# A new order of steps in a two-layer MoE kernel after Nystrom attention

## The chip, the cores and the metric

The kernel runs on one core of a Trainium2 chip. Its time is device microseconds of one execution, as a median over runs. The engines are TensorE (PE, with its weight loads PEld), VectorE (DVE), ScalarE (ACT), GpSimd (POOL) and SyncE (SP), which here only issues transfers. Each has a queue of its own that it works off in order; semaphores hold an instruction back until what it reads has been written and what it overwrites has been read.

## The reference

Inputs are q, k, v of 4 batches, 8 heads, 576 positions and 64 channels, and four weight matrices. First comes Nystrom attention with 32 landmarks, then two dense layers over 2304 tokens (512 channels, 2048 hidden):

```python
A, Bm, C = sm(q, k_lm), sm(q_lm, k_lm), sm(q_lm, k)     # scaled softmax; *_lm: means over 18 positions
Z = Bm.T / (norm1(Bm) * norminf(Bm) + 1e-6)
for _ in range(6): Z = 2 * Z - Z @ Bm @ Z
x = tokens(A @ Z @ C @ v)                                # 2304 x 512
h = x @ w_in;  x = (h * tanh(softplus(h))) @ w_out       # layer 1
h = x @ w2_in; out = square(maximum(h, 0)) @ w2_out      # layer 2
```

## The kernel before

All products of the two layers are made of three passes: each operand is split in a high part (a rounded copy, ScalarE) and a low part (the difference, GpSimd or VectorE), and PE adds high x high, high x low and low x high. Layer 2 moreover uses a scheme of seven products in place of eight on two by two blocks, so that VectorE makes many sums and differences of blocks.

The order of everything is written out by hand in one string, PROGRAM, of 2638 steps, and a loop runs through it and calls for each step one method, which emits the step's few instructions. A step reads `thing.method`, with a number, then `@` and the kind of PSUM buffer that it takes, then `+n`: so many products with the identity go ahead of the next step that takes a PSUM buffer. As every engine works in order, the place of a step in the string sets its place in its engine's queue. It also sets which buffer it gets: a buffer of each kind goes to the next step that asks, in the order in which buffers were given back.

The things that matter here:

- `a` to `h`: groups of heads of the attention; `B0` to `B2`: the iteration for Z; `F`: attention folded into the first weights.
- `U0` to `U63`: 128 rows or columns of a weight matrix; `d` loads them (SP), `lo`, `st`, `ab`, `cl`, `ad` convert them on ScalarE, VectorE and GpSimd, `hi` and `lw` split them, `sv` stores them to DRAM (SP).
- `p0` to `p31`: chunks of 288 tokens of layer 1's hidden part: `f` products, `M` the activation and `c` the high part (ScalarE), `g` the low part (VectorE). `t0` to `t23`: turns of 384 tokens of its second product: `y` on PE (L931 to L933), `e` adds on VectorE (L1016).
- `W0` to `W7`: pairs of layer 2's first weights: `v` sums (VectorE, L1031), `h` high parts (ScalarE, L1039), `l` low parts (GpSimd, L1043), `sv` stores to DRAM (SP, L1051 to L1056), which gives the buffers back. There are four buffers of this kind, "T". `K0` to `K7` do the same for the second weights.
- `X0` to `X2`: the forms of layer 1's output, for three passes of 768 tokens: `t` (VectorE), `h` (ScalarE, L1077), `l` (L1082).
- `Q00` to `Q27` (pass, then pair): the first product of layer 2. `a` loads a 256 KB weight (SP, L1273), `p` is a product (PE, L1284 to L1286, six matmuls), `s` and `d` move its result out of PSUM (ScalarE L1294, VectorE L1314). In pass 0 `r`, `h`, `g` make the activation and its parts, and `y` is the second product (PE, L1357 to L1359); `Q07.e` copies its sums (L1368), and `Q07.o` stores them (SP, L1376).
- `Y10` to `Y22`: the second product of passes 1 and 2: `r` the activation and `t` the sums (VectorE, L1150, L1155), `h` (ScalarE, L1173), `l` (GpSimd, L1178), `b` loads a 256 KB weight (SP, L1184), `p` is a product (PE, L931 to L933, 18 matmuls), `a` adds it to the totals (L1201, L1204).
- `Z1`, `Z2`: the endings of the passes: `u` sums (L1224), `f` (L1234, L1237), `e` and `o` stores.
- `x.e` and `x.m` load ScalarE's tables ahead of use.

The loads `a` and `b` and the split weights share 24 buffers of kind "w"; a load waits until the PE step that last read its buffer is done.

Of the kernel before, what the change touches and what calls it, by code (L numbers as in the profile page):

```python
# [10 lines left out]
F32 = mybir.dt.float32  # L11
F32R = mybir.dt.float32r
U32 = mybir.dt.uint32
# [41 lines left out]
    U0.cl U3.lo B0.n0@at B0.r0 B0.z0 U8.d U4.cl U3.st U4.ad B0.n1@y b.ae U3.ab B0.r1 B0.z1 c.xq U8.lo U4.hi U4.lw c.zq
    b.su U3.cl B0.n2@at B0.r2 B0.z2 b.pe@h c.TL c.pc@h+1 b.ET d.lk d.sk b.mu c.pb@at B0.n3@y B0.r3 b.lv B0.z3 b.pv@y
    U3.ad c.PB b.tb B0.n4@y B0.r4 e.lk c.pa@at B0.z4 c.cm B0.n5@y e.lq c.ce c.at B0.z5 d.tk@h+2 d.Sk b.ah d.tl@y
    e.tk@h c.am e.sq b.cv c.mi d.Tk B0.pw@y B0.wz d.TL U7.ab d.pc@at U5.d U5.lo d.cm c.pe@h e.Tk U0.ad d.pb@y d.PB
    c.ae F00.fo@h+1 B1.bx B1.be d.lv U5.st B1.bs B1.nr@y+1 b.al d.ce d.pe@at U8.st U5.ab B1.rs B1.n0@y U5.cl B1.z0
    F00.mh c.ET F00.ml f.lk f.tk@h U8.ab d.ET U6.d@gh B1.r0 U6.lo U6.st d.pa@at c.cr d.at B1.n1@y B1.z1 U7.cl f.Tk  # L60
    U5.ad U5.hi U6.ab e.Sq B1.r1 U6.cl U6.ad p0.f0 p0.f1 p0.f2 p0.M0 B1.n2@y B1.z2 B1.r2 p0.f3 p0.M1 p1.f0 U7.ad
    B1.n3@y g.lv U6.hi U6.lw d.am f.lq f.sq B1.r3 B1.z3 e.tq@h f.tq@at U7.hi e.Tq e.sk c.lv f.Tq B1.n4@y B1.r4 U7.lw
    B1.z4 p0.c0 p0.g0 d.pv@y f.lv p0.c1 d.cr e.Sk p1.f1 p1.M0 f.Sq c.pv@y c.cv c.su B1.n5@at x.m p1.f2 B1.z5 U5.lw
    e.tl@y p1.c0 p1.g0 p1.f3 p0.g1 d.cv B1.pw@y e.TL e.pb@at B1.wz p1.M1 p1.c1 e.pc@h e.PB F10.fo@h U11.d U11.lo U8.cl
    U8.ad p1.g1 t0.y0 F10.mh t0.y1 d.mi d.ae f.sk e.cm f.Sk e.ce f.tl@at t0.e0 d.su e.pe@h f.TL f.pb@y f.pa@at U9.d
    U9.lo F10.ml t0.e1 U11.st c.mu c.tb c.ah U11.ab f.PB U9.st U9.ab d.mu d.tb d.ah c.al f.pc@h f.cm f.ce t0.y2 t0.e2
    t0.y3 e.ET t0.e3 d.al p2.f0 p2.f1 U11.cl U11.ad g.lq f.at f.am U9.cl e.pa@at e.at p2.M0 p2.c0 p2.g0 g.lk p2.f2
    p2.f3 U9.ad p2.M1 p2.c1 p3.f0 e.am p3.f1 p2.g1 t1.y0 p3.M0 p3.c0 U10.d U10.lo U10.st p3.f2 U10.ab U10.cl g.tk@at
    g.Tk U13.d g.sk t1.e0 U13.lo U10.ad U13.st t1.y1 f.pe@h f.ET t1.y2 F01.fo@h t1.e1 g.Sk U13.ab e.mi e.ae g.tq@at
# [30 lines left out]
    t12.e1 t12.y2 U29.d U29.lo U29.st U35.d U29.ab U35.lo U35.st U35.ab W0.l0 W0.sv0 p18.M0 W0.h1 W0.l1 t12.y3 t12.e3  # L100
    U35.cl p18.M1 p18.c0 p18.g0 p18.c1 U35.ad p19.f0 W0.sv1 p19.f1 p19.f2 p19.f3 t12.e2 p19.M1 F22.fo@at F22.mh p18.g1
    U29.cl U41.d t13.y0 t13.e0 F22.ml W1.v0 W1.v1 W1.h0 p19.M0 p19.c0 t13.y1 t13.e1 U29.ad U29.hi W1.v3 U29.lw W1.v2
    p20.f0 W1.l0 W1.sv0 t13.y2 t13.y3 U40.d p19.g0 F32.fo@at p19.c1 p19.g1 U41.lo t13.e3 W1.h1 W1.l1 W1.sv1 U41.st
    U41.ab t14.y0 t14.e0 p20.f1 p20.f2 t13.e2 p20.f3 U41.cl p20.M0 t14.y1 t14.y2 F32.mh F32.ml p20.c0 p20.g0 U40.lo
# [1355 lines left out]
```

## Time and profile before

| | |
|---|---|
| median of 3 runs | 809.32 us (808.58 to 809.92) |
| profiled execution | 807.2 us |
| its span | 805.4 us |
| mean granted PE clock | 0.993 |
| busy: PE, DVE, ACT, POOL | 771.5, 608.6, 374.9, 383.3 us |
| transfers | 156.73 MB, mean 195 GB/s |

Attention and layer 1 take roughly the first half of the span, layer 2 the second. The busy time of PE is modelled from starts, so two matmuls that follow each other overlap in it; the idle time before an instruction, with the engine that ended it, is what to read for waits.

### The profile page before, as it was taken

How to read it: one execution, taken by the hardware profiler on the slowest of the kernel's cores; microseconds unless marked ns; L12 is line 12 of the kernel's file. 1: busy time of each engine (PE TensorE's matmuls, PEld its weight loads, DVE VectorE, ACT ScalarE, POOL GpSimd, SP SyncE). 2: the span in 40 equal slices, each digit the busy share in tenths (PEclk: the TensorE clock that was granted, in tenths of full speed). 3: DMA queues.
4: the chain of work that ended last, by engine and by line, in shares of the span. 5: the costliest groups of instructions: out<-in, count | busy, mean ns of one | idle time of the engine just before them, and what ended most of it. 6: DMA issues, size and time to landing. Idle time of an engine off the chain costs nothing.

```text
span 805.4 us, 15441 instructions
## 1 busy us (share of the span) xinstructions
PE 771.5 (96%) x5938; PEld 712.9 (89%) x5938; DVE 608.6 (76%) x964; ACT 374.9 (47%) x622; POOL 383.3 (48%) x265
## 2 busy tenths in 40 slices
...
GB/s 329 214 194 142 109 138 110 54 31 75 131 79 88 127 160 164 216 213 252 204 173 254 292 270 256 290 305 267 220 251 281 218 248 210 169 252 306 329 81 79
DMA packets 87721, 156.73 MB, mean 195 GB/s; under 512 B 9184, under 2 KB 37088, under 8 KB 87648
## 3 DMA queue, kind: packets, MB, share of 16 engines
...
## 4 chain that ended last, share of the span: by engine, by line
PE 69%; DVE 12%; POOL 7%; issue 6%; ACT 3%; DMA 2%; SPq 0%; POOLq 0%; ACTq 0%; DVEq 0%
PE y L931 7%; PE y L933 7%; PE y L932 7%; PE P L1284 5%; PE P L1285 5%; PE P L1286 5%; PE hc L931 4%; PE hc L932 3%; PE hc L933 3%; PE O L932 3%; PE O L931 3%; PE O L933 3%; PE O L1359 3%; PE O L1358 3%; PE O L1357 3%
## 5 line engine op out<-in xcount | busy, mean ns | idle before, releaser
L1178 POOL TENSOR_TENSOR ringglx<-A,ringghx 128x768 fp32r<-128x768 f32 x40 | 76.2, 1923 | 63.6 <-ACT ringghx L1173 60.1
L932 PE MATMUL O<-b,ringghx 128*128 128x256 f32 x240 | 68.6, 286 | 3.7 <-DMA b<-sc 3.7
L982 DVE TENSOR_TENSOR ringglx<-sc,ringghx 128x576 fp32r<-128x576 f32 (+2 forms) x80 | 60.1, 775 | 14.8 <-ACT ringghx L977 14.6
L931 PE MATMUL O<-b,ringghx 128*128 128x256 f32 x240 | 68.4, 285 | 1.7 <-DVE sum L1204 1.7
L933 PE MATMUL O<-b,ringglx 128*128 128x256 f32 x240 | 68.6, 286 | 1.1 <-POOL ringglx L1178 1.1
L1016 DVE TENSOR_TENSOR acc<-acc,y 128x384 f32<-128x384 f32 x72 | 39.0, 547 | 36.8 <-PE y L933 36.6
L964 ACT ACTIVATE sc<-hc 128x576 f32<-128x576 f32 x64 | 41.7, 652 | 51.1 <-PE hc L933 31.4
L1173 ACT CAST ringghx<-A 128x768 fp32r<-128x768 f32 x40 | 32.8, 836 | 69.6 <-PE O L932 22.7
L1314 DVE TENSOR_TENSOR U<-U,P 128x384 f32<-128x384 f32 x72 | 39.6, 551 | 33.8 <-PE P L1286 32.2
L932 PEld LDWEIGHTS O<-b,ringghx 128*128 128x128 f32 x240 | 46.5, 194 | 4.0 <-DMA b<-sc 4.0
L977 ACT CAST ringghx<-sc 128x576 fp32r<-128x576 f32 (+2 forms) x80 | 44.2, 578 | 12.2 <-PE y L933 11.4
L1314 DVE TENSOR_TENSOR A<-U,P 128x384 f32<-128x384 f32 x56 | 30.2, 548 | 25.8 <-PE P L1286 21.3
L931 PEld LDWEIGHTS O<-b,ringghx 128*128 128x128 f32 x240 | 46.4, 193 | 2.1 <-issue 2.0
L933 PEld LDWEIGHTS O<-b,ringglx 128*128 128x128 f32 x240 | 46.5, 194 | 1.3 <-POOL ringglx L1178 1.3
L404 POOL TENSOR_TENSOR wi<-rawwi 128x512 int32<-128x512 int32 x16 | 20.3, 1271 | 47.2 <-DVE rawwi L398 38.4
L1294 ACT COPY U<-P 128x384 f32<-128x384 f32 x24 | 11.5, 480 | 63.8 <-PE P L1286 53.9
L1204 DVE TENSOR_TENSOR sum<-sum,O 128x768 f32<-128x768 f32 x32 | 30.1, 949 | 10.5 <-PE O L933 10.4
L1155 DVE TENSOR_TENSOR A<-A,A 128x768 f32<-128x768 f32 x28 | 34.4, 1227 | 2.3 <-POOL ringglx L1178 1.8
L1150 DVE SCALAR_TENSOR_TENSOR A<-A 128x768 f32<-128x768 f32 x28 | 35.7, 1298 | 0.3
L418 POOL TENSOR_TENSOR rawwo<-rawwo 128x512 int32<-128x512 int32 x14 | 16.9, 1207 | 35.9 <-DVE rawwo L398 27.2
L411 POOL TENSOR_TENSOR wa<-rawwi 128x512 int32<-128x512 int32 x16 | 17.4, 1093 | 30.8 <-DVE rawwi L398 24.5
L384 DVE SCALAR_TENSOR_TENSOR rawwi<-rawwi 128x512 uint32<-128x512 uint32 x32 | 24.3, 764 | 10.0 <-ACT rawwi L381 10.0
...
## 6 DMA issues: line engine op xcount, KB each, us to landing
...
```

What stands on the lines that cost most here:

```text
L931: nc.tensor.matmul(ps, wh, rh, start=start, stop=False)
L932: nc.tensor.matmul(ps, wh, rl, start=False, stop=False)
L933: nc.tensor.matmul(ps, wl, rh, start=False, stop=stop)
L964: nc.scalar.activation(s, self.hs[hf][:, :, :CH], AF.Mish)
L977: nc.scalar.copy(self.at_ring("gh", hf, c0, e - a), self.s[hf][:, :, a:e])
L982: nc.vector.tensor_tensor(lo, self.s[hf][:, :, a:e], hi.bitcast(F32), ALU.subtract)
L1016: nc.vector.tensor_tensor(a, a, ps, ALU.add)
L1178: nc.gpsimd.tensor_tensor(lo, self.A[self.src(k)], hi.bitcast(F32), ALU.subtract)
L1284: nc.tensor.matmul(ps[:, :TT], wh[:, c], xh[:, c, :], start=c == 0, stop=False)
L1285: nc.tensor.matmul(ps[:, :TT], wh[:, c], xl[:, c, :], start=False, stop=False)
L1286: nc.tensor.matmul(ps[:, :TT], wl[:, c], xh[:, c, :], start=False, stop=c == 1)
L1314: nc.vector.tensor_tensor(to, x, self.ps[i][:, :TT], ALU.add)
```

## The change

The string PROGRAM is replaced by another with the same 2638 steps, each with the same kind of PSUM buffer; the methods and all else stay as they are. The numbers behind `+` stand at other places (before, 13 products with the identity in all; after, 19). On PE a step moves by 1.4 places in the mean and 17 at most; VectorE's by 2.9 and 37, GpSimd's by 1.7 and 20, SP's by 11.7 and 128. ScalarE changes its tables at as many places in both. The diff, cut to the stretches that are spoken of below (layer 1's last third; the beginning of layer 2; the end of pass 0; pass 1, with its last blocks):

```diff
-    t16.y2 U49.cl W3.v2 W3.l0 W3.sv0 U49.ad W4.v0 U48.cl t16.e2 W3.h1 W3.l1 W3.sv1 t16.y3 t16.e3 p24.M0 p24.f2 p24.f3
...
-    Q12.p3 U63.sv Q07.e2 Y10.l0 Q07.y0 Q07.y4 Y10.b1 Q07.e3 Q07.o3 Q12.d4 Q07.y5 Y10.h1 Q12.d5 Q12.d7 Y10.h3 Y10.l3
-    Y10.b11 Q13.p5 Q13.d4 Q07.e0 Q13.p3 Q07.e1 Y11.b2 Y10.b13 Y10.p4@h Y10.b4 Q13.d5 K7.h0 Q07.e4 Q07.e5 K7.l0 Y10.t2
...
-    Q22.a2 Y12.l4 Y12.p6@at Y13.t1 Q21.a3 Q20.a2 Q20.p1 Q20.p2 Q20.s Q20.d1 X2.l4 Q20.a5 K7.sv1 Q21.a0 Q20.a3 Q20.a4
...
-    Q21.p7 Q21.d2 Q21.d3 Y13.l1 Y13.t4 Q21.a1 Q21.p4 Y13.b7 Y13.b10 Y13.b13 Y13.p5@h Y12.a3 Y20.r0 Q23.a4 Y13.h5
...
-    Q22.p5 Q24.a3 Y13.h6 Q22.d4 Q22.d5 Q22.p3 Z1.f5 Q22.d7 Z1.f4 Y13.b4 Z1.u5 Q23.a2 Y13.b5 Y13.l6 Y13.p3@at Q23.a0
...
+    t16.e0 x.e W3.h0 W3.v2 W3.v3 W3.l0 F03.mh U49.lo F03.ml W3.sv0 W3.h1 W3.l1 W3.sv1 t16.e1 p23.M0 p23.c0 U49.st
+    U49.ab Q02.a3 U49.cl U49.ad U48.ad t16.y2 p23.c1 p24.f0 p23.g0 t16.e2 p23.g1 p24.f1 p24.M0 p24.f2 p24.f3 W4.v0
...
+    Q01.a0 Q04.a1 t23.e3 Q00.p1 U44.ab X0.l3 U44.cl X0.h6 X0.l6 Q00.p2 Q00.a3 Q00.p6@h Q00.s U44.ad Q00.d1 Q01.a2
...
+    Q07.e0 U62.sv Q07.e1 Q13.d2 Y10.r2 K6.sv1 Y10.h5 Q07.e2 Y10.l5 Q07.y4 Q20.a2 Q07.e3 Q07.y5 Q13.a6 Q13.p7 Q13.d3
+    Q13.d4 Y10.h1 Y10.h3 Y10.l3 K7.sv0 Y10.l1 Q07.e4 Q07.e5 Y10.b13 Q13.d5 Y10.p4@h Q12.p3 Q12.d7 Q15.a1 Q13.p3 Q13.p4
...
+    Y12.p3@h Y13.t2 Q21.p2 Y13.t4 Q21.a3 Y20.b6 Q21.d1 Q21.a5 Q21.p6 Q21.d2 Q21.p7 Y13.h4 Q21.p5 Q21.d3 Q21.d4 Y13.l4
+    Y13.b12 Q21.p4 Q21.d6 Y13.h3 Y13.h5 Y13.b7 Y13.b8 Y13.p6@h Y12.a3 Y12.a6 Y13.l2 Q21.d5 Y20.r3 Q21.p3 Q21.d7 Y13.a6
+    Y20.r1 Q22.p2 Q22.d1 Q22.a1 Y13.l3 Y13.p4@h Y13.h6 Y13.b6 Y13.p5@h Y13.a5 Y20.h2 Z1.u2 Y13.b11 Y20.r2 Y13.l5
+    Y13.p7@at Y20.h1 Y13.l6 Q22.a4 Y13.a7 Z1.u3 Q07.o1 Q22.a6 Y20.t1 Y20.h3 Y13.b3 Y13.b5 Q22.a3 Q22.a5 Q22.p6 Q22.d2
...
```

Of VectorE's queue the prediction also uses: ahead of Q20.d1, behind Q17.d7, the new order has Y13.r2 and Y12.t4; ahead of Q14.d1, behind Q13.d7, it has Y11.r1, Y10.t2, Y10.t4, Y11.r3, Y11.r0, Y11.r2, Y11.t1 and Y11.t3 (before: Y10.t4, Y11.r2, Y11.r3, Y11.r1, Y11.t1, Y11.r0). On PE, Q13.p4 is followed there by Y10.p5, Y10.p1, Y10.p2, Q14.p1, Y10.p7, Q14.p2, Y11.p4, Q14.p6 and Q14.p7.

## Rows read from the trace of the kernel before

**Rows 1.** The page, part 1: busy us, share of the span, instructions.
```profile
PE 771.5 (96%) x5938; PEld 712.9 (89%) x5938; DVE 608.6 (76%) x964; ACT 374.9 (47%) x622; POOL 383.3 (48%) x265
```
**Rows 2.** Waits of PE: waiting line, releaser: us in total, times, longest us.
```profile
PE P L1284 <- DVE A L1314: 5.8, 4, 3.5
PE O L932 <- DMA b<-sc: 3.7, 1, 3.7
PE hc L931 <- ACT sc L964: 2.5, 2, 2.3
...
PE O L931 <- DVE sum L1204: 1.7, 1, 1.7
...
PE O L933 <- POOL ringglx L1178: 1.1, 1, 1.1
```
**Rows 3.** A window after the 2.3 us wait; PEclk is third from last.
```profile
326.52:329.93 3.41, 3.41 (x22) 2.06 (x7) 1.72 (x4) 2.26 (x3) 0.59 (x2) 0.50 0.85 271
```
**Rows 4.** Timelines at 561 to 576 us: start, us, instructions [idle before <-releaser].
```profile
561.38 0.38 SPq L1184 DMA_DIRECT2D b<-sc  x1
568.85 1.75 SPq L1376 DMA_DIRECT2D out_dram<-o  x4
570.70 2.77 SPq L1184 DMA_DIRECT2D b<-sc  x6
...
568.24 0.59 ACT L1368 COPY o<-O 128x512 f32<-128x512 f32 x1 [7.09 <-DVE o L1368]
...
575.68 0.58 PE L932 MATMUL O<-b,ringghx 128*128 128x256 f32 x1 [3.74 <-DMA b<-sc]
```
**Rows 5.** Loads of the Q weights, line L1273: issue to landing.
```profile
DMA to landing us min/median/max: 2.5/4.2/7.7
```
**Rows 6.** Timelines of SP, ACT and PE at 314 to 326 us.
```profile
319.94 0.42 SPq L1053 DMA_DIRECT2D st<-wa  x1
...
322.15 1.05 ACT L1039 CAST wh<-ws 128x1024 fp32r<-128x1024 f32 x1 [2.77 <-DMA st<-wa]
...
325.22 0.40 PE L931 MATMUL hc<-three0x,mh 128*128 128x288 f32 x1 [2.32 <-ACT sc L964]
```
**Rows 7.** Timelines of DVE, POOL and PE at 651 to 661 us.
```profile
653.40 4.09 DVE L1150 SCALAR_TENSOR_TENSOR A<-A 128x768 f32<-128x768 f32 x2
657.42 2.56 DVE L1155 TENSOR_TENSOR A<-A,A 128x768 f32<-128x768 f32 x1
659.90 0.54 DVE L1314 TENSOR_TENSOR A<-U,P 128x384 f32<-128x384 f32 x1
...
654.12 2.56 POOL L1082 TENSOR_TENSOR three0x<-t,three3x 128x768 fp32r<-128x768 f32 x1
656.64 2.52 POOL L1082 TENSOR_TENSOR three2x<-t,three1x 128x768 fp32r<-128x768 f32 x1
...
660.50 0.44 PE L1284 MATMUL P<-three3x,q20w 128*128 128x384 f32 x1 [3.52 <-DVE A L1314]
```
**Rows 8.** PE's timeline: successive matmuls of a Q step and of Y13.p4.
```profile
571.31 0.33 PE L1285 MATMUL P<-three2x,q13w 128*128 128x384 f32 x1
571.49 0.33 PE L1286 MATMUL P<-three2x,q13w 128*128 128x384 f32 x1
...
682.17 0.28 PE L932 MATMUL O<-b,ringghx 128*128 128x256 f32 x1
682.29 0.28 PE L933 MATMUL O<-b,ringglx 128*128 128x256 f32 x1
```
**Rows 9.** The page, part 5: line L1155, busy us, mean ns of one.
```profile
L1155 DVE TENSOR_TENSOR A<-A,A 128x768 f32<-128x768 f32 x28 | 34.4, 1227 | 2.3 <-POOL ringglx L1178 1.8
```
**Rows 10.** Timelines of DVE and POOL at 678 to 698 us.
```profile
678.39 2.57 DVE L1155 TENSOR_TENSOR A<-A,A 128x768 f32<-128x768 f32 x1 [1.80 <-POOL ringglx L1178]
680.89 0.94 DVE L1204 TENSOR_TENSOR sum<-sum,O 128x768 f32<-128x768 f32 x1
...
693.15 4.43 POOL L1224 TENSOR_TENSOR sum<-sum,sum 128x768 f32<-128x768 f32 x2 [13.00 <-DMA out_dram<-o]
```

More of the change, by code (lines that the diff above doesn't have):

```diff
@@ L55 @@
[L55 to L69, printed above, removed]
@@ L100 @@
[L100 to L104, printed above, removed]
@@ L170 @@
-    Q15.p5 Y11.b13 Y11.b0 Y11.p1@h Y11.h4 Y11.a1 Y11.p4@h Y11.a4 Y11.b11 Y11.h6 Q15.a6 Q15.p7 Q15.d3 Y11.l6 Y10.a6
-    Q17.a6 Q15.d4 Q15.d5 Y12.r3 Y10.p3@h Y11.h5 Y11.l5 Y10.a3 Y11.b6 Y11.b3 Y11.p2@at Q07.o1 Y11.a2 Q17.a3 Y11.b8
-    Q15.p3 Q15.a1 Q15.p4 Q15.d6 X2.h0 Y12.r2 Y11.b10 Q15.d7 Y11.p7@h Y12.h1 Y12.r1 Q16.a0 Y12.t1 Y11.l4 Y11.b9
-    Y11.p6@at Y12.h3 Y11.a6 K7.sv0 Y11.a7 Y12.t3 Y11.b7 Y11.p5@h Y12.l3 Q16.a2 Y12.h2 Y12.l2 Y11.b5 Y11.a5 Q16.p1
-    Q16.p2 Q16.s Y12.b2 Q16.d1 Q17.a2 Q17.p1 Q17.a4 Q17.s X2.t0 X2.l0 Y11.b4 Y13.b2 Q17.p2 Y11.p3@h Y11.a3 Q17.d1
@@ new lines @@
+    W4.v1 W4.v3 F13.fo@at F13.mh t16.y3 t16.e3 W4.v2 W4.h0 W4.h1 W4.l0 p25.f0 p25.f1 t17.y0 t17.e0 U50.d t17.y1 t17.e1
+    Q00.a4 t17.y2 F13.ml p24.M1 p24.c0 p24.c1 U51.d W4.sv0 p24.g1 t17.e2 p24.g0 p25.M0 U51.lo U51.st U51.ab t17.y3
+    Q00.a6 p25.f2 p25.f3 p26.f0 p26.f1 p25.c0 U50.lo p25.M1 p25.c1 p25.g0 U50.st U51.cl W4.l1 W4.sv1 Q04.a4 t17.e3
+    p26.f2 U51.ad W5.v0 p25.g1 U50.ab U50.cl p26.M0 U50.ad W5.v1 p26.f3 p26.M1 W5.v2 t18.y0 t18.y1 t18.e1 t18.e0 U56.d
+    W5.v3 F23.fo@at W5.h0 W5.l0 t18.y2 t18.e2 t18.y3 U56.lo U56.st Q02.a0 p26.c0 U56.ab U56.cl p26.c1 U56.ad p26.g0
@@ new lines @@
+    Q04.p2 Q04.d1 K4.t3 Q04.p6 Q04.d2 U55.d Q04.p5 U55.lo U55.st U54.d Q02.y3 Q04.p7 U55.ab U55.cl U46.hi K3.l0 K3.sv0
+    K4.t4 Q03.h1 Q03.g1 K4.h1 K4.l0 K4.sv0 Q10.a0 K1.h1 U47.lw Q04.d3 Q04.d4 U47.sv Q04.d5 U54.lo U54.st Q02.y4 Q02.y5
+    U46.lw Q03.y3 U55.ad Q04.p4 Q04.d6 Q07.a5 Q06.a6 Q04.p3 Q04.d7 Q04.r0 Q03.y4 Q05.p2 Q05.a3 Q05.p6 U46.sv Q04.r1
+    K4.l1 Q04.h0 Q05.a1 Q04.g0 Q05.d1 Q05.d2 Q03.y1 K2.h1 K1.l1 Q11.a2 U54.ab Q05.p7 K1.sv1 K2.l1 Q05.d3 Q05.p5 U53.hi
+    U53.lw Q04.h1 Q04.g1 Q10.a3 U60.d Q05.d4 Q05.d5 U54.cl Y10.b7 U52.hi U52.lw Q05.p4 U54.ad K5.t1 K5.t2 Q03.y2
@@ new lines @@
+    Q05.d6 X1.t0 U60.lo X1.h0 Q05.p3 Q03.y0 K3.h1 Q05.d7 Q03.y5 Q06.a0 Q05.r0 Q05.h0 Q06.a3 Q06.a5 Q06.a1 Q05.r1
+    Q05.h1 U60.st U54.hi Q06.p1 Q05.g0 Q06.s Q06.p2 Q06.d1 Q04.y3 Q04.y0 K2.sv1 Y11.b0 Q07.a0 K5.t3 Q06.a4 K3.l1
+    Q06.p6 Q04.y4 Q06.d2 K5.t4 K5.h1 U60.ab U60.cl U54.lw Q05.g1 U61.d Q07.p1 Q07.s K3.sv1 X1.l0 U61.lo U61.st U53.sv
+    U60.ad K5.l1 Q06.p7 Q14.a6 Q06.d3 Q06.p5 Q06.d4 Q06.d5 U55.hi U55.lw K4.sv1 Q04.y2 U61.ab X1.t1 X1.h4 U61.cl
+    Q06.p4 Q06.d6 U61.ad Q04.y1 Q05.y1 Q06.p3 Q06.d7 Q06.r0 U52.sv Q11.a0 Q04.y5 U62.d U62.lo Q06.r1 U55.sv Q06.h0
@@ new lines @@
+    Q11.p1 Q11.s Q06.g0 U63.d Q05.y4 Q10.a2 X1.h1 Q07.p2 Q07.d1 Q07.p6 Q07.a6 Q07.a4 Q10.p1 Q10.s Q13.a4 Q05.y3 Q07.d2
+    K6.t3 X1.t2 Q07.p7 K5.sv1 Q07.d3 K6.t1 K6.t2 K6.t4 X1.t3 X1.l1 Q10.p2 Q11.p2 Q11.d1 Q10.d1 U60.hi Q10.a4 U60.lw
+    Y10.b2 Q05.y0 U60.sv Q07.p5 U61.hi Q07.d4 Q07.p4 Q11.a5 K6.h0 U61.lw K6.l0 Q10.a1 Q05.y2 Q06.h1 Q06.g1 X1.l4
+    Q06.y0 Q07.d5 Q07.p3 U54.sv U62.st Q05.y5 Q07.d6 Q07.d7 K5.h0 K5.l0 Q10.a5 Q10.p6 Q10.d2 Q11.a3 Q11.p6 Q10.a6
+    X1.h5 X1.l5 Q10.p7 K5.sv0 X1.h3 X1.l3 Q11.d2 Y11.b6 Q10.p5 K6.sv0 Q10.d3 X1.h6 X1.l6 Q10.d4 Q10.d5 U63.lo Q12.a3
@@ new lines @@
+    U63.st Q06.y2 U62.ab Q10.p4 X1.l2 U62.cl Q06.y4 Q10.d6 Q10.p3 K6.h1 Q13.a0 Q13.a2 Q13.p1 Q10.d7 Q11.a6 Q11.a4
+    Q11.p7 Q13.s Q14.a1 U62.ad Q06.y1 Q07.r0 Q07.h0 Q12.a1 U63.ab U63.cl Q11.a1 Q07.r1 Q07.h1 Q11.p4 Q11.d3 Q11.d6
+    Q13.p2 Q13.d1 U63.ad K6.l1 Q13.a5 Q12.p1 Q12.s Q12.p2 Q12.d1 Q11.p3 Q11.p5 Q11.d4 U61.sv Y12.b12 Q11.d5 Q11.d7
+    Y10.r1 Q12.a6 Q07.g0 Q12.a4 K7.t1 K7.t3 K7.t2 Q06.y3 Q12.a5 Q12.p6 K7.t4 Q12.p5 Q12.d2 U63.hi U63.lw U63.sv U62.hi
+    K7.h0 U62.lw Q14.a2 Q06.y5 Y11.b5 Q07.g1 Q07.y1 Q12.p7 Q12.d3 Q12.d4 Y10.b12 Q12.d5 Q17.a3 Q07.y0 Q12.p4 K7.l0
```

252 lines of the change are left out of this document (124 added, 128 removed).

## The prediction, made before the changed kernel was run

> **What bounds the kernel now.** I read the page's busy shares first, then the waits of TensorE, then the timeline around the longest of them, then the landing times of the transfers. TensorE (PE) is busy 771.5 of 805.4 us [rows 1], so its instructions are the floor, and an order of the same instructions can only move the 33.9 us in which it is not busy, and what its clock loses. The list of its waits [rows 2] shows where: five places in the middle and late part hold 3.7 (a transfer), 2.3 (ScalarE), 3.5 and 1.7 (VectorE) and 1.1 us (GpSimd), 12.4 us together. The reader is to see that each is a queue with something unhurried at its head, not an engine without time. After a long wait the granted clock stands at 0.50, the 1.2 GHz level, for the 3.41 us of [rows 3]. PE's columns there take twice as long, so such a wait costs some 1.7 us more. It is so after the waits of 3.7, 2.3 and 3.5 us; I charge 1.7 to each of these and nothing to shorter ones. The profiled execution took 807.2 us (span 805.4), 2.1 under the median of 809.32; I sum against 807.2 and add 2.1.
>
> **Outputs of layer 1 in the transfer queue: a gain of 5.0.** SP issues in order. It stood from 561.4 to 568.9 us before Q07.o3, whose copy Q07.e3 ScalarE ran only at 568.24; behind it stood Y10.b13, which therefore landed late, and PE waited for it until 575.68 [rows 4]. The new order puts Q07.o3 39 us of PE work behind its copy, and no Q07.o and no Z1.o within 9 us of its copy; nothing of that kind stands ahead of Y10.b13. Its cover is gone in another way, though: the buffer of Y10.b13 now comes free with Q13.p5, and until Y10.p4 PE has only Q07.y4, Q07.y5 and Q13.p7, 3.8 us. Weight transfers land 4.2 us after their issue in the median, 2.5 at best and 7.7 at worst [rows 5]. So 3.74 + 1.7 goes and 0.4 comes back: -5.0 (bounds: -5.4 with a landing under 3.8; -1.5 with the worst one, 3.9 late, the clock kept).
>
> **GpSimd's subtractions and their transfers in layer 1's end: a gain of 4.0.** W3.h1 on ScalarE waited 2.77 us for the transfer of W3.sv0 to land, as it takes the buffer that this frees; p24.M0 stood behind it, and PE waited 2.32 us for p24.M0 [rows 6]. In the new order U49.ad comes after W3.h1, not ahead of it, so W3.h1 takes the buffer freed by W2.sv1, a store earlier. W2.h1 still takes one freed by W2.sv0, as before; PE has 8.8 us of work there where it had 10.9 (a step t.y is 12 products of 0.175), and W2.v2 stands one sum earlier, so I cost that at nothing. -2.3 - 1.7 = -4.0 (bounds -4.0 and 0).
>
> **VectorE's order in layer 2: a gain of 3.2.** Q20.d1, which PE's Q20.p7 needs, stood behind Y13.r1, Y13.r2 and Y13.t1. The last two took 2.6 us each beside GpSimd's subtractions, and PE waited 3.52 us [rows 7]. In the new order Y13.r2 and Y12.t4 stand there: one slow sum of 2.5 less, 1.0 left, and the clock is kept: -4.2. But five sums (Y13.r1, t1, t3, t2, t4) now stand together ahead of Q21.d1. From the end of Q20.p3 PE has Q21.p1, Q22.p1, Y12.p3, Q21.p2, Q21.p6 before Q21.p7 needs it: 6 products at 0.175 us for each Q step, 18 at 0.12 for Y12.p3 [rows 8], 4 x 1.05 + 2.16 = 6.4. VectorE needs Q20.d7 and Q21.d1, 1.1, and five sums: at their mean of 1.23 [rows 9] 7.2 in all, 0.8 late, I take +1.0; at 0.95 each 5.9, not late; at 2.56 each 13.9, 7.5 late, and 1.7 for the clock. I take the mean, as it is over the whole of layer 2. Eight such sums ahead of Q14.d1 (there were six) have 13.8 us of PE work as cover against 8 x 1.23 + 1.6 = 11.4: nothing, but 8.3 if each takes 2.56.
>
> The rows show a sum at 2.56 beside a subtraction at 2.56, the two ending in turn. The Trainium skill ("SBUF — State Buffer", SBUF: two separate sides) says that a VectorE operation with two SBUF inputs and a GpSimd operation that reads SBUF take a shared port in turn, each for the whole instruction. By it a run of sums among ready subtractions always pays 2.56, which is the dear end above; by the mean row half of them meet none.
>
> **Two late links of layer 2: a gain of 2.8.** Y12.a3 stood behind Y13.t4, 2.57 us long, and PE waited 1.7 for it; Y13.l6 stood on GpSimd behind Z1.u7 and Z1.u5, 4.43 us, and PE waited 1.1 [rows 2, 10]. In the new order Y12.a3 is well behind Y13.t4's stretch, with Y13.p6 as the product ahead of Y13.p4, and Y13.l6 comes before Z1.u7. Both go: -2.8 (bounds -2.8 and 0).
>
> **Layer 2's transfers: a loss of 2.5.** The 24 weight buffers are handed out in the order in which they come free, so a load can't start before the PE step that last read its buffer, nor before the loads ahead of it on SP. I counted PE's work from that step to the one that needs the load, in both orders: of 274 loads 2 had under 6 us, now 15 have, and the median falls from 18 to 14. The shortest but Y10.b13: Q00.a3 3.1, Q04.a3 4.8, seven of 5.2 to 5.3, five of 5.5 to 5.9. Against the median of 4.2 only Q00.a3 is late, 1.1; of the rest some land over it, for which I put 1.4. Bounds: 0, or 10 with every such load landing at 5.9 (2.8 at Q00.a3, 1.1 at Q04.a3, 0.7 at six separate places, and 2.0 at Y10.b13).
>
> **The rest: a loss of 5.5.** The identity products that fill PE in the first 65 us go from 13 to 19; each is two passes of 128 columns, about 0.12, ahead of products that mostly wait: +0.5 (0 to 1.4). And an order made anew has late links that I did not find: of its 33.9 us without work PE has 21.5 outside the five named places, and I charge the new order for two places of about 1.7 and one fall of the clock: +5 (0 to 15).
>
> **Sum.** -5.0 - 4.0 - 3.2 - 2.8 + 2.5 + 5.5 = -7.0: 800.2 for the profiled execution, 802.3 against the median.
>
> **The rivals.** *Loads late (slower).* The mechanism is the 15 short leads, the place 400 to 600 us, where the 256 KB loads stand close. For it: the median lead falls by 4 us and the worst landing is 7.7. Against it: in the order before, loads with leads of 4.5 and 5.3 made no wait that the list shows. It decides from a landing of about 5.9: then 10 in place of 2.9, and two falls of the clock, 3.4: 802.3 + 7.1 + 3.4 = 813.
> *VectorE in turn with GpSimd.* If both runs of sums pay 2.56 each, Q21.p7 is 7.5 late in place of 1.0, Q14.p7 8.3 in place of nothing, and two falls of the clock add 3.4: 802.3 + 18 = 820 at its worst. One of the two, the likelier form, is 802.3 + 8 = 810. For it: [rows 7]. Against it: GpSimd is 48% busy over the span [rows 1] and its subtractions stand farther apart in the new order.
> *No change.* The new order has as many late links as the old: the unnamed +5 becomes 12: 809.
> *The waits stay:* if the long waits come from buffers and not from the queues that I named, the moved steps change nothing; that is 809 too, and I count it with the former.
>
> **Chances.** Forecast 0.50 (its own range 796 to 807), loads late 0.18, VectorE in turn 0.14, no change 0.18. About 0.2%, 1.6 us, is what a measurement of this kernel can tell from no change. All of the forecast's cases and 0.09 of the others are faster by more; of "no change" and the 810 case 0.16 lies within it; loads late, the rest of VectorE's case and a part of "no change", 0.25, are slower. The range, 794 to 815, takes in the forecast with its bounds, 813 and 810, and leaves out about 2 in 10.
>
> **What would show it.** Right: no transfer wait of PE over 1 us near Y10.p4; p25.f0 without a wait for p24.M0; Q20.p7 at most 1 us late; Y13.p3 and Y13.p4 without waits over 0.5; the clock lower fewer than three times. Wrong: PE waits for 256 KB loads adding to over 5 us, a wait over 3 us before Q14.p7 or Q21.p7, or waits over 1 us at three or more places not named here.

## The result, and the profile after

The new order takes 784.80 us (median of 4 runs, 784.05 to 786.43); the order before took 809.62 beside it on the same chip (4 runs, 808.58 to 811.32). The ratio is 0.9694, with an interval of 0.9671 to 0.9718. That is 24.8 us less where 7.0 were forecast, and it lies below the forecast range. The profiled execution took 784.31 us with a span of 782.2: 22.9 less than that of before.

TensorE's idle time has shrunk from 33.9 us [rows 1] to 18.8. The page's first part, of the kernel after:

```profile
PE 763.4 (98%) x5952; PEld 713.0 (91%) x5952; DVE 613.6 (78%) x964; ACT 376.1 (48%) x622; POOL 387.0 (49%) x265
```

Waits of PE, kernel after (waiting line, releaser, us in total, times, longest). Lines stand one lower than before. All five places of [rows 2] are gone. The 4.7 us stand at the very start, for the first load, where the order before waited 1.5 and 2.2. The longest wait in the middle is now one within h.pv (L697), which waits for nothing that the profile shows ("issue"); the loads cost 0.5, 0.4 and 0.3:

```profile
PE tk L569 <- DMA ringglx<-in_k_dram: 4.7, 1, 4.7
PE pv L697 <- issue: 3.4, 1, 3.4
PE pc L657 <- ACT qT L624: 1.1, 1, 1.1
PE nw__804 L848 <- DVE inv L838: 0.9, 1, 0.9
PE P L1283 <- DVE C L1313: 0.8, 1, 0.8
PE O L1357 <- POOL wo_4l L432: 0.8, 1, 0.8
PE y L931 <- DVE ringglx L981: 0.8, 1, 0.8
PE P L1283 <- DMA q04w<-st: 0.5, 1, 0.5
PE P L1283 <- DMA q14w<-st: 0.4, 1, 0.4
PE P L1283 <- DMA q00w<-st: 0.3, 1, 0.3
```

Apart from the last 1 to 2 us, at 0.50 in both orders, the clock falls once in place of three times [rows 3], around that wait, but for 6.83 us in place of 3.41 (window; PEclk third from last):

```profile
145.24:152.07 6.83, 5.58 (x86) 4.79 (x86) 3.09 (x7) 0.27 (x1) 2.26 (x2) 0.50 0.01 2
```

*Layer 1's end.* ScalarE's timeline, kernel after: the second row is W3.h1. It has no idle time ahead of it, where [rows 6] had 2.77 us. PE runs p25.f0 at 325.31 without a wait.

```profile
316.48 0.69 ACT L380 ACTIVATE rawwi<-rawwi 128x512 f32<-128x512 uint32 x1
317.05 1.04 ACT L1038 CAST wh<-ws 128x1024 fp32r<-128x1024 f32 x1
```

*The transfer queue.* SP's timeline, kernel after: Y10.b13 (the first row) is issued at 559.65, and no output stands ahead of it, where [rows 4] had Q07.o3. Its data lands at 563.08; PE starts Y10.p4 at 563.46, right behind the step before.

```profile
559.65 0.33 SPq L1183 DMA_DIRECT2D b<-sc  x1
560.07 0.38 SPq L1272 DMA_DIRECT2D q15w<-st  x1
561.90 1.27 SPq L1183 DMA_DIRECT2D b<-sc  x3
```

*VectorE and GpSimd.* Timelines of DVE and POOL, kernel after. Ahead of Q20.d1, Y13.r2 at 637.92 takes 1.12 us and Y12.t4 at 638.97 takes 2.61, beside subtractions. Y13.r1 and the four sums behind it, the run that I feared ahead of Q21.d1, take 0.95 to 1.00 each, because POOL does nothing from 648.70 to 654.53. In [rows 7] two of them, Y13.r1 and Y13.t1, stood beside X2's subtractions. The mean of a sum is 1244 ns over the whole layer, no lower than in [rows 9]: what moved is which sums are slow.

```profile
637.92 1.12 DVE L1149 SCALAR_TENSOR_TENSOR A<-A 128x768 f32<-128x768 f32 x1
638.97 2.61 DVE L1154 TENSOR_TENSOR A<-A,A 128x768 f32<-128x768 f32 x1
641.76 0.56 DVE L1313 TENSOR_TENSOR A<-U,P 128x384 f32<-128x384 f32 x1 [0.18 <-PE P L1285]
...
649.59 0.95 DVE L1149 SCALAR_TENSOR_TENSOR A<-A 128x768 f32<-128x768 f32 x1
650.64 4.00 DVE L1154 TENSOR_TENSOR A<-A,A 128x768 f32<-128x768 f32 x4
```

```profile
638.18 2.58 POOL L1081 TENSOR_TENSOR three2x<-acc,three0x 128x768 fp32r<-128x768 f32 x1
640.72 2.57 POOL L1081 TENSOR_TENSOR three2x<-t,three1x 128x768 fp32r<-128x768 f32 x1
643.24 1.85 POOL L1081 TENSOR_TENSOR fl<-acc,fh 128x768 fp32r<-128x768 f32 x1
645.04 3.66 POOL L1177 TENSOR_TENSOR ringglx<-A,ringghx 128x768 fp32r<-128x768 f32 x2
654.53 1.85 POOL L1177 TENSOR_TENSOR ringglx<-A,ringghx 128x768 fp32r<-128x768 f32 x1 [5.84 <-ACT ringghx L1172]
```

**Where the time went.** I weighed each matmul of both traces by the usual distance from its start to the next one's for its shape, and compared the times at which the same amount of this work is left. The difference between two such places is what the stretch gained, waits and clock included, however the steps in it are ordered. Stretches are named by the time in the trace of before:

| stretch, us | gain | what lies there |
|---|---|---|
| 0 to 315 | -1.9 | 4.9 lost at 130 to 150 (the wait in h.pv), 3.0 gained elsewhere |
| 315 to 335 | 4.2 | p25.f0 behind W3.h1 |
| 335 to 410 | -0.1 | |
| 410 to 560 | 3.7 | small waits of pass 0 |
| 560 to 580 | 5.6 | Y10.p4 behind Q07.o3 |
| 580 to 650 | 2.4 | small waits of pass 1 |
| 650 to 665 | 5.6 | Q20.p7 |
| 665 to 700 | 3.1 | Y13.p4, Y13.p3 |
| 700 to 720 | 1.8 | Q23.p2 behind Q22.d7, 1.5 us: one of the 4 waits in the first line of [rows 2] |
| 720 to the end | -1.0 | a wait for VectorE of 0.8 |
| sum, to the start of the last matmul | 23.4 | |

The small waits of layer 2 are these lines of the order before (waits of PE), seven waits of 0.2 to 0.5 us, none of which [rows 2] shows, and 0.5 and 0.3 more in its first line:

```profile
PE P L1284 <- DVE C L1314: 0.6, 2, 0.4
PE P L1284 <- DVE U L1314: 0.5, 1, 0.5
PE O L933 <- POOL glr L1178: 0.5, 1, 0.5
PE O L1359 <- DVE ringglx L1337: 0.4, 1, 0.4
PE P L1285 <- POOL fl L1082: 0.4, 1, 0.4
PE O L931 <- ACT sum L1201: 0.4, 1, 0.4
```

They weigh more than the list says, as it counts from the modelled end of the matmul before and leaves out the shortest. At 410 to 560 us it has 1.9 us of them, while PE's starts fall behind their usual distances by 6.6 us in all before and by 3.0 in the new order.

### The profile page after: what moved, and what is told of

Its sections match the earlier page's. It is cut to its first block, busy times and chain, and to the rows that moved or that the text cites. A ratio compares the mean times of both kernels' runs of the same rounds, so it can differ in the third digit from the quotient of the medians.

```text
span 782.2 us, 15515 instructions
## 1 busy us (share of the span) xinstructions
PE 763.4 (98%) x5952; PEld 713.0 (91%) x5952; DVE 613.6 (78%) x964; ACT 376.1 (48%) x622; POOL 387.0 (49%) x265
## 4 chain that ended last, share of the span: by engine, by line
PE 93%; DMA 3%; DVE 2%; ACT 1%; issue 1%; SPq 0%; POOL 0%; ACTq 0%; DVEq 0%; POOLq 0%
PE y L930 9%; PE y L931 8%; PE y L932 8%; PE P L1283 7%; PE P L1285 7%; PE P L1284 7%; PE hc L930 5%; PE hc L931 4%; PE hc L932 4%; PE O L932 4%; PE O L931 4%; PE O L930 4%; PE O L1358 3%; PE O L1357 3%; PE O L1356 3%; PE m L912 2%
## 5 line engine op out<-in xcount | busy, mean ns | idle before, releaser
L981 DVE TENSOR_TENSOR ringglx<-sc,ringghx 128x576 fp32r<-128x576 f32 (+2 forms) x80 | 63.5, 820 | 5.3 <-ACT ringghx L976 5.3
L410 POOL TENSOR_TENSOR wa<-rawwi 128x512 int32<-128x512 int32 x16 | 19.0, 1191 | 42.8 <-DVE rawwi L397 39.3
L1154 DVE TENSOR_TENSOR A<-A,A 128x768 f32<-128x768 f32 x28 | 34.8, 1244 | 1.1
L1149 DVE SCALAR_TENSOR_TENSOR A<-A 128x768 f32<-128x768 f32 x28 | 33.1, 1198 | 0.4
L383 DVE SCALAR_TENSOR_TENSOR rawwo<-rawwo 128x512 uint32<-128x512 uint32 x30 | 28.1, 935 | 6.1 <-ACT rawwo L380 6.1
```

What stands on the lines that cost most here:

```text
L981: nc.vector.tensor_tensor(lo, self.s[hf][:, :, a:e], hi.bitcast(F32), ALU.subtract)
```

## The experiments

Times are medians; ratios are to the order before, run beside the kernel, with 95% intervals, and "us" behind a ratio is that share of before's median. The clock also falls at places that differ from one execution to the next: at 39.4 and 148.6 us in b_out's profile and at 51.7 in a_pa_r3's, though the profiles of before and of a_pa_late, whose steps up to there are the same, have no fall at these places. Runs of one kernel spread by up to 1%, and the slower ones have the lower mean clock.

### One named cause at a time, in the order before

**b_out**
```diff
- Y10.b1 Q07.e3 Q07.o3 Q12.d4
+ Y10.b1 Q07.e3 Q12.d4
...
- Y10.b13 Y10.p4@h
+ Y10.b13 Q07.o3 Y10.p4@h
```


> The order before, with one transfer moved: Q07.o3 goes from its place right behind its copy Q07.e3 to right behind Y10.b13. Theory A (each named wait is a queue with something unhurried at its head): the PE wait of 3.74 us ahead of Y10.p4 goes, the clock does not fall there, 5.4 us less, about 804. Rival B (the gain lies in the new order as a whole; one moved step only hands the wait on to the next late link): Y10.p4, or a step right behind it, waits over 2 us for another transfer or for VectorE, and the time is 808 to 810.

Measured: 804.79 us, ratio 0.9942 (0.9918 to 0.9965), 4.7 less. Y10.p4 has no wait; SP still stands 3.6 us before the store, and 1.2 come back at Y10.p1. This is Theory A.

**b_sub**
```diff
- W3.sv0 U49.ad W4.v0 U48.cl t16.e2 W3.h1 W3.l1 W3.sv1
+ W3.sv0 U48.cl t16.e2 W3.h1 U49.ad W3.l1 W3.sv1 W4.v0
```


> The order before, with U49.ad (GpSimd) moved behind W3.h1, and W4.v0 (VectorE), which reads what it writes, behind W3.sv1. Theory A: W3.h1 no longer waits for the landing of W3.sv0, PE's wait of 2.3 us at p25.f0 goes and the clock stays up behind it, 4.0 us less, about 805.5. Rival B: the wait comes back within 10 us, at W4's steps or at p25 or p26, and the time is 808 to 810.

Measured: 805.84 us, ratio 0.9952 (0.9933 to 0.9972), 3.9 less; no wait at p25.f0 and none within 10 us behind it. This is Theory A.

**b_sums**
```diff
- Y13.r1 Y13.h2 Y13.r2 Y12.b8 X2.l1 Q22.a2 Y12.l4 Y12.p6@at Y13.t1
- Q21.a3 Q20.a2 Q20.p1 Q20.p2 Q20.s Q20.d1 X2.l4
+ Y13.r1 Y13.h2 Y12.b8 X2.l1 Q22.a2 Y12.l4 Y12.p6@at
+ Q21.a3 Q20.a2 Q20.p1 Q20.p2 Q20.s Q20.d1 Y13.r2 Y13.t1 X2.l4
...
- Y13.t4 Q21.a1 Q21.p4 Y13.b7 Y13.b10 Y13.b13 Y13.p5@h Y12.a3
+ Q21.a1 Q21.p4 Y13.b7 Y13.b10 Y13.b13 Y13.p5@h Y12.a3 Y13.t4
...
- Z1.u5 Q23.a2 Y13.b5 Y13.l6
+ Q23.a2 Y13.b5 Y13.l6 Z1.u5
```


> The order before, with VectorE's and GpSimd's queues changed at three places of layer 2: Y13.r2 and Y13.t1 go behind Q20.d1, Y13.t4 behind Y12.a3, Z1.u5 behind Y13.l6. Theory A: the waits of 3.5 us (Q20.p7), 1.7 (Y13.p4) and 1.1 (Y13.p3) go, and with the first the fall of the clock (1.7): 8.0 us less, about 801.5. Rival B: VectorE has no time to spare there, the sums put off are late for Y13.h1, Y13.h5 or Z1.f5, and PE waits for these: at most 3 us less, 806.5 or more.

Measured: 808.63 us, ratio 0.9974 (0.9952 to 0.9996), 2.1 less. This is Rival B. The waits at Y13.p4 and Q20.p7 are gone and that at Y13.p3 too, but Y13.t1 is as slow behind Q20.d1 as it was ahead of it, and the wait moves one step on, to Q20.p5. Timelines of DVE, POOL and PE, kernel b_sums (Y13.t1 is the 2.58; the POOL row is X2.l6):

```profile
659.44 0.98 DVE L1150 SCALAR_TENSOR_TENSOR A<-A 128x768 f32<-128x768 f32 x1
660.35 2.58 DVE L1155 TENSOR_TENSOR A<-A,A 128x768 f32<-128x768 f32 x1
662.84 1.20 DVE L1314 TENSOR_TENSOR U<-U,P 128x384 f32<-128x384 f32 x2
...
659.57 2.53 POOL L1082 TENSOR_TENSOR three2x<-t,three1x 128x768 fp32r<-128x768 f32 x1
...
663.44 0.44 PE L1284 MATMUL P<-three3x,q20w 128*128 128x384 f32 x1 [2.47 <-DVE U L1314]
```

With Z1.u5 later, the three slow sums of Z1.f5 (5.64 us) still stand ahead of Q22.d7, and Q23.p2 waits 2.9 us in place of 1.5.

**b_all3**, the three edits together:

> The order before, with the moves of the three kernels before this one together (6 of 2638 steps moved that were named as causes, and W4.v0 that has to follow). Theory A: the gains add, 5.4 + 4.0 + 8.0 = 17.4 us less, about 792, some 7 us above the changed kernel; these 7 are then small waits that the new order takes away elsewhere. Rival B: 804 or more, and the changed kernel's gain lies in its order as a whole.

Measured: 799.37 us, ratio 0.9882 (0.9830 to 0.9934), 9.6 less; the three alone add up to 10.7. So the gains add, within the interval, but that of the sums is a quarter of what Theory A put there.

**b_all3b**, against b_all3:
```diff
- Q20.d1 Y13.r2 Y13.t1 X2.l4
+ Q20.d1 X2.l4
...
- Q20.p7 Y13.h1 X2.l3
+ Q20.p7 X2.l3
...
- Q20.p3 Q20.d7 Q21.a2 Q21.p1 Q21.s Q21.p2 Y13.h3 Y13.l3
+ Q20.p3 Q20.d7 Y13.r2 Y13.t1 Q21.a2 Q21.p1 Q21.s Q21.p2 Y13.h3 Y13.h1 Y13.l3
```


> The order before with the moves of b_all3, except that Y13.r2 and Y13.t1 go farther back: not just behind Q20.d1 but behind Q20.d7, past the last of GpSimd's subtractions for X2 (Y13.h1 follows them). b_all3 kept a PE wait of 2.5 us at Q20.p5 and a fall of the clock, with Y13.t1 at 2.57 us beside X2.l6. Theory A (the sums are slow only beside GpSimd's subtractions, and it is these that have to be avoided, not one place in the queue): Y13.r2 and Y13.t1 take 0.95 each, the wait goes, 4 to 5 us less than b_all3: 794 to 796. Rival: VectorE has no place for them; the sums are then late for Y13.h3 or Q21.d1, and the time stays at 799.

Measured: 801.51 us, ratio 0.9914 (0.9881 to 0.9947): no better than b_all3. Half of Theory A holds: Y13.r2 and Y13.t1 take 0.95 there and the wait at Q20.p5 is gone. But Y13.l0 now comes late behind X2's subtractions (PE waits 1.8 at Y13.p1), Y13.t2 meets Y13.l3 and takes 2.56 (1.3 at Q21.p6), and the 2.9 at Q23.p2 stays. In this stretch each fix shows the next link; both queues have to be laid out anew together.

### One named cause put back, in the new order

**a_out_undo**
```diff
- Q07.e3 Q07.y5
+ Q07.e3 Q07.o3 Q07.y5
...
- X2.t0 Q07.o3 Y11.l5
+ X2.t0 Y11.l5
```


> The new order with Q07.o3 put back right behind its copy Q07.e3, 73 steps earlier. Theory A: SP stands before it from 558.2 until the copy is done at 563.0, the load of Y10.b13 is issued some 5 us later, and PE waits 4 to 5 us for it at Y10.p4, with a fall of the clock: 789 to 792. Rival: the loads behind it have time to spare in the new order, under 1.5 us more, 785 to 786.

(It is 127 steps earlier, not 73.) Measured: 794.65 us, ratio 0.9819 (0.9792 to 0.9847): 9.8 above the new order's 784.8, more than both expected. SP's timeline, the waits of PE at 560 to 580 us and a window behind them, kernel a_out_undo: SP stands from 557.2 to 564.4; Q13.a6 right behind it is late first, by 5.1, and Y10.b13 by another 1.7. The clock is at 0.50 for 6.82 us.

```profile
556.89 0.33 SPq L1272 DMA_DIRECT2D q20w<-st  x1
564.37 1.77 SPq L1375 DMA_DIRECT2D out_dram<-o  x4
566.23 0.37 SPq L1272 DMA_DIRECT2D q13w<-st  x1
```

```profile
PE P L1285 <- DMA q13w<-st: 5.1, 1, 5.1
PE O L931 <- DMA b<-sc: 1.7, 1, 1.7
```

```profile
569.53:576.35 6.82, 5.09 (x21) 4.69 (x21) 2.17 (x4) 0.59 (x1) 0.50 (x1) 0.50 0.75 254
```

Taking this store away from ahead of Y10.b13 gains 4.7 us in the order before (5.6 in the table of stretches), and putting it there costs 9.8 in the new one. SP stands 7.1 us both times; PE waits 3.7 us in the one and 6.8 in the other, with 3.4 and 6.8 us at 0.50 behind it. The shorter leads of the loads are the reason that fits the rows: they cost little while SP keeps moving, and leave no cover when it stops. No run changes the leads alone.

**a_sums_undo**
```diff
- Y13.b13 Q24.a1 Y13.b10 Q20.d1
+ Y13.b13 Q24.a1 Y13.b10 Y13.r1 Y13.t1 Q20.d1
...
- Q21.s Y13.r1 Y13.t1 Y13.t3
+ Q21.s Y13.t3
```


> The new order with Y13.r1 and Y13.t1 put back ahead of Q20.d1, where they stand beside GpSimd's subtractions X2.l6 and X2.l5 again. Theory A: each takes some 2.5 us there in place of 0.95, Q20.d1 is late by about 4, PE waits 3 to 4 us at Q20.p7, the clock falls once: 788 to 790. Rival (VectorE has time to spare there, the order of the sums hardly counts): under 1.5 us more, 785 to 786.

Measured: 792.33 us, ratio 0.9800 (0.9767 to 0.9833), 7.5 above the new order. This is Theory A, with a wait and a fall of the clock (6.81 us at 0.50) larger than expected. DVE and PE, kernel a_sums_undo: the same Y13.r1 and Y13.t1 that took 0.95 and 1.00 take 2.58 and 2.44.

```profile
641.91 2.58 DVE L1149 SCALAR_TENSOR_TENSOR A<-A 128x768 f32<-128x768 f32 x1
644.53 2.44 DVE L1154 TENSOR_TENSOR A<-A,A 128x768 f32<-128x768 f32 x1
646.89 0.54 DVE L1313 TENSOR_TENSOR A<-U,P 128x384 f32<-128x384 f32 x1
...
647.49 0.69 PE L1283 MATMUL P<-three0x,q20w 128*128 128x384 f32 x1 [4.37 <-DVE A L1313]
```

### The new order in one stretch only

Each of these is a prefix of one order and the remaining steps in the other order. The cuts lie at W3.v1 (300 us), at Q16.s or Y11.a6 (612 us) and at Y13.h6 (695 us).

**h_first_before**: before up to W3.v1, then the new order.

> Steps up to W3.v1 (some 300 us) in the order before, all later steps in the new order. The two traces start t15.y0 at 298.6 and 299.0 us. Theory: the gain of 24.8 us is made behind that point, in layer 1's last third and in layer 2, by waits that the new order of those steps does not have: about 784.5. Rival: the gain needs the new beginning too (which buffer goes to whom is settled there, and all later waits hang on it): 792 or more.

Measured: 785.54 us, ratio 0.9699 (0.9666 to 0.9732), 24.4 less. As the theory says, the gain is made behind 300 us.

**h_first_after**: the new order's first 300 us, then the order before.

> The opposite: the steps of the first 300 us in the new order, all later steps in the order before. Theory: nothing gained, 809 to 811, with the waits of 2.3, 3.7 and 3.5 us back at p25.f0, Y10.p4 and Q20.p7. Rival: a good part of the gain stays, 803 or less.

Measured: 812.92 us, ratio 1.0029 (1.0007 to 1.0052), 2.3 more, somewhat over the theory. The three waits are back (4.2, 4.0 and 3.4 us), and the wait in h.pv, 3.4 us, comes on top.

**cut_mid**: before, the new order from W3.v1 to Y11.a6, before.

> The order before up to W3.v1 (300 us), the new order from there to Y11.a6 (some 612 us), then the order before again. Theory S (the gain is spread, as the starts of PE's matmuls in the two traces say: 15 us between 300 and 612 us, 9 between 612 and 696, 1 behind it, and the stretches don't depend on each other): about 15 us less, 795. Rival N (all but the named waits is a property of the whole order): only the named waits of this stretch go, 4.0 at p25.f0 and 5.4 at Y10.p4: 800 or more.

Measured: 796.90 us, ratio 0.9829 (0.9805 to 0.9853), 13.9 less. This is Theory S: more than the named 9.4. Behind 600 us the waits of PE, kernel cut_mid, are those of [rows 2] again:

```profile
PE P L1283 <- DVE A L1313: 6.6, 4, 3.5
PE O L930 <- DVE sum L1203: 1.7, 1, 1.7
PE O L932 <- POOL ringglx L1177: 1.1, 1, 1.1
```

**cut_late**: before up to Q16.s, then the new order.

> The order before up to Q16.s (some 612 us), all later steps in the new order. Theory S: some 10 us less, 799 to 801, with no wait of over 1 us at Q20.p7, Y13.p4 and Y13.p3. Rival N: as moving single steps there gave 1.5 to 2 us, the new order of this stretch alone, with another beginning, gives under 5: 805 or more.

Measured: 803.58 us, ratio 0.9916 (0.9891 to 0.9942), 6.8 less: between the two. The waits at Y13.p4 and Y13.p3 are gone and that at Q20.p7 is down to 0.7 us, while one of 1.3 for VectorE has come up at Q17.p1, 22 us behind the join.

**cut_end**: before up to Y13.h6, then the new order.

> The order before up to Y13.h6 (some 695 us), all later steps in the new order. Theory S: 0 to 1.5 us less, 808 to 810. Rival N: 805 or less would mean that the end holds a good part of the gain.

Measured: 811.16 us, ratio 1.0001 (0.9983 to 1.0020). The end holds nothing.

Together: 13.9 + 6.8 + 0.0 - 2.3 = 18.4 of 24.8 us. Some 6 us exist only when neighbouring stretches are both new. h_first_before, where all behind 300 us is new, gains 24.4, which is 3.7 more than 13.9 + 6.8, so that much belongs to the join at 612 us; the work left in the traces puts about 4 of it at 580 to 665 us. The other 2.7 would belong to the join at 300 us, and the intervals are as wide as that. Which links these are I did not settle.

### The one wait that the new order adds

PE stands for 3.42 us within h.pv, among products of 7 ns distance. Timeline of PE, kernel after, and the transfer queues (kind, packets, MB, share) at 139.3 to 143.9 and at 143.9 to 145.0 us:

```profile
142.32 0.75 PE L697 MATMUL pv<-three3x,ET 96*32 96x64 f32 x37
146.49 0.64 PE L697 MATMUL pv<-three3x,ET 96*32 96x64 f32 x11 [3.42 <-issue]
```

```profile
q1 hardware_dynamic: 411, 1.54, 98.3%
...
q1 hardware_dynamic: 21, 0.04, 8.7%
q8 instruction: 1, 0.02, 5.3%
```

The queue q8 brings instructions, 16 KB at a time: 47 transfers in the span, so one for about 127 of the 5952 products. Here 256 products lie between the fetches at 134.4 and at 143.98. Ahead of the second, three weight loads (1.5 MB), which h.pa had released, filled the transfer engines.

**a_pa_late**
```diff
- B2.n0@at B2.r0 B2.z0 h.pa@h+1 B2.n1@y
+ B2.n0@at B2.r0 B2.z0 B2.n1@y
...
- t4.e0 h.at B2.z2 h.am g.pv@y
+ t4.e0 B2.z2 g.pv@y
...
- h.pv@y U30.ab U24.d@T B2.n4@at B2.z4 p7.f2
+ h.pv@y h.pa@h+1 U30.ab U24.d@T B2.n4@at B2.z4 h.at h.am p7.f2
```


> The new order with one change at 138 us: h.pa goes behind h.pv, and h.at and h.am, which read it, behind B2.z4. PE's stretch of small products stays as dense as it was, but the three weight loads of 512 KB each that wait for h.pa start some 5 us later. It is for the wait of 3.42 us within h.pv, in which PE waits for nothing that the profile shows, while the fetch of 16 KB of PE's instructions starts at 143.98, as the loads end. Theory L (the fetch stands behind the loads): the fetch starts by 141.5, the wait is under 0.5, the clock does not fall to 0.50 there, and the time is about 778. Theory D (256 small products in 9 us use up instructions faster than any fetch brings them, loads or not): the wait is 3 us or more, about 785.

Measured: 780.50 us (779.93 to 783.02), ratio 0.9641 (0.9607 to 0.9675), under the new order's in all 4 runs. The fetch starts at 141.51, with no load under way (the queues at 141.4 to 143.0 us, and PE's timeline, kernel a_pa_late); h.pv's 48 products run through at the old density, and the clock does not fall anywhere between 9 and 777 us. This is Theory L. The change also takes h.pa's 18 products out of the stretch; the next kernel leaves them there.

```profile
q8 instruction: 1, 0.02, 5.2%
```

```profile
142.22 0.88 PE L697 MATMUL pv<-three3x,ET 96*32 96x64 f32 x48
```

**a_spread**
```diff
- t4.e0 h.at
+ t4.e0 t4.y1 h.at
...
- B2.n3@y B2.z3
+ B2.n3@y p7.f2 t4.e1 B2.z3
...
- B2.n5@at g.mu
+ B2.n5@at t4.y2 t4.e2 g.mu
```


> The new order with big products moved in among the small ones: t4.y1 ahead of g.pv and p7.f2 ahead of h.pv, 3.2 us of PE work, with t4.e1 ahead of B2.z3 and t4.y2 and t4.e2 behind B2.n5; h.pa and the loads stay. Theories L and D both expect PE at the end of its instructions 3 us later and the wait of 3.42 us cut to 0.5 or less, about 778 to 779; a rival, that the wait belongs to h.pv's own operands, keeps it ahead of h.pv with 3 us or more, 785.

Measured: 783.27 us, ratio 0.9667 (0.9635 to 0.9698), not the 778 to 779 expected. The wait is gone, the fetch still starts only as the loads end (144.62), which also speaks for L. But B2.pw has lost its filler (1.6 us), three small waits stand beside it (0.8, 0.5, 0.4), and little is gained: the place is right, the cure is the dearer one.

**after_again, pa_late_again, a_pa_r3**, side by side; the third also has Y22.r3 behind Q25.d6:
```diff
- Y21.b10 Y22.r3 Q26.p2
+ Y21.b10 Q26.p2
...
- Q25.d6 Q25.p3
+ Q25.d6 Y22.r3 Q25.p3
```


> The new order once more, beside the next two. Theory L: 784 to 786, with the wait of 3.4 us within h.pv and the clock at 0.50 behind it.

> The new order with h.pa, h.at and h.am late, once more. Theory L: no wait in h.pv, and 4 to 6 us less than the new order in the same job. Rival: the gain of 4.3 us seen in another job was chance, and the two lie within 1.5 us.

> The same with one more step moved, Y22.r3 behind Q25.d6. In a_best this was the one of three moves whose wait (0.83 us at Q25.p3) went without another in its place. Theory: 0.8 to 1.0 us under pa_late_again, at the limit of what the runs can tell.

Measured: 785.16, 782.15 and 781.26 us; ratios 0.9676 (0.9650 to 0.9702), 0.9642 (0.9615 to 0.9669), 0.9626 (0.9599 to 0.9653). The late h.pa gives 3.0 us here, less than expected, and 4.3 above. The last step's 0.9 is as expected, but within the spread.

**a_best**: a_pa_late with Y22.r3 as above and
```diff
- B2.z4 h.at h.am p7.f2 f.su p7.g0 f.mu B2.r4 B2.n5@at
+ B2.z4 h.at p7.f2 B2.r4 B2.n5@at B2.z5 h.am p7.g0 f.su f.mu
...
- t22.y2 X0.t2 t22.y3
+ t22.y2 t22.y3
...
- p31.g1 t23.y0
+ p31.g1 X0.t2 t23.y0
```


> The new order with h.pa, h.at and h.am late as in a_pa_late, and three more steps moved that stand at the head of a queue ahead of one for which PE waits: B2.z5 goes ahead of h.am, p7.g0 and f.su (PE's wait of 0.74 us at B2.pw), X0.t2 behind p31.g1 (0.79 at t23.y0), Y22.r3 behind Q25.d6 (0.83 at Q25.p3). Theory A: all three waits go and the time is 2.0 to 2.4 us under a_pa_late's 780.5, about 778. Rival (each is handed on to the next late link): 780 to 781.

Measured: 780.87 us, ratio 0.9655 (0.9629 to 0.9680). This is the rival: the wait at B2.pw turns up as 1.2 us at F20.fo, the one at t23.y0 stays near by; only Y22.r3's goes.

## Why the prediction was wrong

What it said of single places held. All its signs of being right came in: no wait over 1 us for a transfer near Y10.p4, none at p25.f0, Q20.p7, Y13.p3 and Y13.p4, fewer than three falls of the clock. By the letter one sign of being wrong came in too, waits over 1 us at three places not named: 4.7 at the first load, 3.4 in h.pv and 1.1 at L657. Only that in h.pv is a new place; the other two stand in the list of before, with 2.2 and 1.1. The sum failed, by its last terms. Gains of the profiled execution, from the table of stretches:

| step of the prediction | forecast | measured |
|---|---|---|
| outputs in the transfer queue | -5.0 | -5.6 |
| subtractions at layer 1's end | -4.0 | -4.2 |
| VectorE's order (Q20.d1, Q21.d1) | -3.2 | -5.6 |
| two late links | -2.8 | -3.1 |
| loads with shorter leads | +2.5 | +1.2 |
| "The rest: a loss of 5.5" | +5.5 | -6.1 |
| sum | -7.0 | -23.4 |

**The step that failed** is "an order made anew has late links that I did not find", charged as +5. With the +0.5 for the identity products it is the term called "the rest"; its -6.1 are the stretches that no other term names (-3.7 - 2.4 - 1.8 + 1.9 + 0.1 + 1.0 = -4.9) without the 1.2 for the loads. Of the 16.4 us of the miss, 11.6 are this term. The runs show the opposite: cut_mid gains 13.9 us where its named waits account for 9.4, and the traces show 3.7 us less at 410 to 560, 2.4 at 580 to 650 and 1.8 at 700 to 720. The new order has one late link of size, the wait in h.pv, and it is not one that a wait list of before, read as queues of the engines, would show: before had it with 1.5 us at the same fetch. No row spoke for a loss of this kind; five of five named places had changed for the better, and small waits of the same kind stood all over layer 2. One was not even small: Q23.p2's 1.5 us, more than the fifth place that I named, stood inside the first line of [rows 2]. Zero, with the bound open to both sides, is what the rows allowed. That the small waits went is read from the traces; none of them was moved by itself.

**VectorE's order** was too small by 2.4. I took the mean of 1.23 for each of five sums; they took 0.95 to 1.00, since GpSimd was idle just then, and the 1.0 charged for them did not come. Nor did the 1.0 left at Q20.p7: Y13.r2, ahead of it, took 1.12 in place of 2.6. A sum here costs 0.95 alone, about 2.5 in the midst of GpSimd's subtractions, and something between where it meets the end of one (1.0 to 2.3 in the traces of the two orders). Which of these it is, is settled by what GpSimd does at that moment: 0.95 and 1.00 in the new order, 2.58 and 2.44 for the same two steps in a_sums_undo. The mean over a layer is the price of none of them. The Trainium skill's rule ("SBUF — State Buffer", SBUF: two separate sides), which I set aside in favour of the mean, is what the trace agrees with: 2.5 beside a GpSimd operation, 0.95 without.

**The clock** was priced at 1.7 for each fall. That holds for the three of before. After the waits of 3.42 us (h.pv), 4.4 (a_sums_undo) and 5.1 with 1.7 (a_out_undo) it stayed at 0.50 for 6.8 us, which costs 3.4; as 3.52 and 3.74 in the order before had 3.41 behind them, the length of the wait alone doesn't settle it. One kernel shows both: the wait in h.pv, 3.55 us in after_again's profile, had 3.41 us behind it there (window, kernel after_again):

```profile
148.52:151.93 3.41, 3.41 (x66) 2.93 (x66) 2.00 (x5) 0.27 (x1) 0.63 (x1) 0.50 0.02 5
```

Nor is the charge of nothing for shorter waits safe: b_out's falls at 39.4 and 148.6 us came with waits of 1.1 and 1.8 us, where before's 1.1 and 1.5 at these places had none.

**The rivals.** Loads late: the leads did shrink, but the loads waited for in the list add up to 1.2 us; a_out_undo shows what the short leads are bad for. VectorE in turn with GpSimd: real as a mechanism, but the new order steers clear of it. No change, and waits that stay: the first is refuted by the time, the second by b_out and b_sub.

**Alone and together.** The cases of SP and of layer 1 could be had by moving one step (4.7 and 3.9). That of VectorE could not (2.1 of 8.0, and b_all3b no better), though putting it wrong in the new order costs 7.5: I predicted the removal of a wait as if the rest of its stretch were free.
